# Projecting the MLP before the query: w3 ahead of wq, and x issued by ScalarE beside the first load

## The chip, the core and the metric

The kernel runs on one core of a Trainium2 chip. The metric is the device time of one execution in microseconds (us), median of several runs. A profile of one execution gives, for the same program, when each instruction started, what ended each wait, and every packet that the sixteen DMA engines of the core moved.

TensorE is PE in the profile, VectorE is DVE, ScalarE is ACT, GpSimd is POOL and SyncE is SP. PEld is the weight load of TensorE. A name with a q behind it (SPq, ACTq) is the sequencer of that engine, which issues DMAs and waits on semaphores.

## What is computed

One decoding step for two rows x of 1024 numbers, all in fp32. An attention branch with a long cache and an MLP branch are mixed by a gate:

```
g  = sigmoid((x * gate_w).sum(-1))
q  = x @ wq                                   # 1024 x 4096: 32 heads of 128
p  = softmax(q k^T * 128**-0.5)               # 4 key/value heads, 32768 positions, 2 batch rows
a  = (p v) @ wo                               # 4096 x 1024
b  = x1 + gelu(layernorm(x1) @ w3) @ w4       # w3 1024 x 3584, w4 3584 x 1024
out = g * a + (1 - g) * b
```

With a sequence of one, the spatial shift of the reference moves zeros in, so x1 is x, and w1 and w2 are not needed.

## The kernel before

The work is a stream of large loads through two buffers. `ring` holds two buffers of 64 KB in each of 128 partitions (8 MB each), called `flat[0]` and `flat[1]` when seen as flat rows. In order, they take wq in two halves, w3 in two halves, then for each of the eight pairs of batch row and key/value head the cache k in two halves and the cache v in two halves (`kt`, `vt`), with w4 in two halves after four pairs, and at the end wo. wq, k and v halves fill a buffer; a half of w3 or w4 takes seven eighths of one. What doesn't fit of wo goes to `tail`.

All these loads are issued by SP, one after the other. Before each, SP waits until the buffer that it overwrites has been read: `at("q0")`, `at("h0")`, `at("k0", m)` are counts on TensorE's semaphore that are reached when a half has been multiplied. A load is thus issued when TensorE is done with the load two places ahead of it, and runs behind the load that is then still under way in the other buffer.

The prologue (everything ahead of the eight pairs) is written out by hand, each engine's instructions in program order, with semaphores between them:

- The first two loads (`early`, L245) are issued by SP inside the tile context. Closing that context makes the engines meet twice at a barrier (L249). The next loads and all else come after it.
- x and gate_w lie in one small array `xg` (128 partitions of 96 bytes). Its DMA was issued by ACT behind the barrier (L278).
- When x has landed, DVE, PE and ACT work out the gate g, the layer norm and the padded operands: `x_pad` (x itself, for wq), `xn_pad` (the normed x, for w3) and `xr_pad` (x times 1 - g, which starts the sum in `acc`). The last of these on DVE is L338, `d_norm`.
- `project` multiplies one weight matrix, half by half, 32 matmuls a half. It takes the landing of a half off its semaphore and, when done with it, marks the semaphore for which SP waits. A float32 matmul stands as two records in the profile, so a half is 64.
- Before: q (x by wq), then the turn of q into columns (DVE L402 and L410, PE L416, DVE L424 and L427, which ends with `q_cur`, the operand of the first pair); then eight matmuls of `xr_pad` into `acc` (L434); then h (normed x by w3), its turn (L438 to L453) and the gelu (L457 to L469). Both turns go through the same buffers `row` and `p`.
- After the prologue the first pair multiplies `q_cur` by the first half of k as soon as that has landed (L488).

Of the kernel before, what the change touches and what calls it, by code (L numbers as in the profile page):

```python
# [14 lines left out]
P = 128  # L15
B, D, HQ, HKV, SK, DH, F = 2, 1024, 32, 4, 32768, 128, 3584
REP = HQ // HKV
PAIRS = B * HKV
# [8 lines left out]
PART = 2  # L27
HALF = P // PART
# [45 lines left out]
def kernel(  # L74
# [52 lines left out]
    nc = tc.nc  # L127
    scale = DH ** -0.5

    def new(name, *shape, parts=P):  # L130
        return nc.alloc_sbuf_tensor(name, [parts, *shape], F32).ap()

    def bank(name):
        return nc.alloc_psum_tensor(name, [P, 512], F32).ap()
# [3 lines left out]
    xg_sb = new("xg_sb", KD, 3)  # L138
    wide = new("wide", 3 * P)
    ones = new("ones", P)  # L140
    x_pad = new("x_pad", KD, C)
    xn_pad = new("xn_pad", KD, C)
    xr_pad = new("xr_pad", KD, C)
    q_pad = new("q_pad", PAIRS + 1, PART, 2, C)
    q_cur = new("q_cur", PART, 2, C)
# [19 lines left out]
    h = new("h", 2 * KF * B)  # L165
    u = new("u", 2 * KF * B)
# [5 lines left out]
    p = new("p", NI, NT, PART + 1, HALF)  # L172
# [4 lines left out]
    row = pt_all[:, 0]  # L177
# [6 lines left out]
    sc = [bank(f"sc{i}") for i in range(NI)]  # L184
    tr = [bank(f"tr{i}") for i in range(2)]
# [5 lines left out]
    compact = ident[:, ::C // B]  # L191
# [3 lines left out]
    def sem(name):  # L195
        cleared.append(nc.alloc_semaphore(name))
        return cleared[-1]

    stored = nc.alloc_semaphore("stored")
    pe, dve, act, pool = (Line(e, sem(n)) for e, n in (  # L200
        (nc.tensor, "pe"), (nc.vector, "dve"), (nc.scalar, "act"), (nc.gpsimd, "pool")))
    sp = Line(nc.sync)

    landed = [sem(f"landed{i}") for i in range(2)]
    w_in = [*landed, sem("w_in2")]
    got_x = sem("got_x")
# [10 lines left out]
    def load(dst, src, sem, *marks):  # L217
        sp.after(*marks)
        nc.sync.dma_start(dst, src).then_inc(sem, 16)

    def run(src, j):
        return src[PART * j:PART * (j + 1)].rearrange("i (q w) c -> (i q) (w c)", w=PART)

    flat = [t.rearrange("p w c -> p (w c)") for t in ring]

    PROLOGUE = ("run", "sum", "var", "q0", "q1", "qt", "h0", "h1", "ht")
    TURN = ("k0", "v0", "v1")
    STEP = ("s0", "s2", "s3", "mt", "bp", "tp00", "tp01", "tp02", "tp03", "tp10", "tp11", "tp12", "tp13", "lp", "op")  # L230

    def at(name, m=None):
        if m is None:
            return (pe.sem, 1 + PROLOGUE.index(name))
        return (pe.sem, len(PROLOGUE) + m * len(TURN) + m // 4 * 2 + 1 + TURN.index(name))

    def weighed(i):
        return (pe.sem, len(PROLOGUE) + 4 * len(TURN) + 1 + i)

    SUMMED = (pe.sem, len(PROLOGUE) + PAIRS * len(TURN) + 2 * 2)  # L240
    ENDED = (pe.sem, SUMMED[1] + 1)

    early = [nc.sync.dma_start(flat[j], run(wq, j)).then_inc(landed[j], 16) for j in range(2)]  # L245
    for inst in early:
        tc.no_tile_sem_insts.add(inst.ins.name)
    tc.close()
    tc.compile()  # L249

    load(flat[0][:, :PART * 2 * F], run(w3, 0), landed[0], at("q0"))
    load(flat[1][:, :PART * 2 * F], run(w3, 1), landed[1], at("q1"))

    half = PART * KF // 4
    STEPS = ((0, 14), (14, 9), (23, 5))
# [5 lines left out]
            load(flat[j][:, piece], run(src, j)[:, piece], landing, free[j])  # L261

    for m in range(PAIRS):
        free = [at("h" + "01"[j]) if m == 0 else at("v" + "01"[j], m - 1) for j in range(2)]
        if m == 4:
            weights(w4, ((0, half), (half, half)), *free)
            free = [weighed(0), weighed(1)]
        for j in range(2):
            load(flat[j], run(kt[m], j), landed[j], free[j])
        for j in range(2):  # L270
            load(flat[j], run(vt[m], j), landed[j], (at("k0", m), (k1_free, m + 1))[j])
    weights(wo, STEPS, at("v0", PAIRS - 1), at("v1", PAIRS - 1))
    load(tail[:, :2 * D], run(wo, 0)[:, half * D:], came[0][0])
    for mark, lo, hi in zip(came[1:], (0, 5, 7), (5, 7, 8)):
        load(tail[:, 2 * D + lo * D // G:2 * D + hi * D // G], run(wo, 1)[:, half * D + lo * D // G:half * D + hi * D // G], mark[0])


    nc.scalar.dma_start(xg_sb, xg).then_inc(got_x, 16)  # L278
    pool.mark(nc.gpsimd.memset(wide, 0.0))
    pool.after((pool.sem, pool.n))  # L280
    made = pool.mark(nc.gpsimd.affine_select(
        out=ident, in_=ident, pattern=[[-1, P]], base=0, channel_multiplier=1,
        compare_op=ALU.not_equal, fill=1.0))
# [17 lines left out]
    for i in range(2):  # L301
        last = nc.vector.tensor_copy(perm[:, :, i], ident.rearrange("p (q w) -> p w q", w=PART))
# [12 lines left out]
    for i in range(2):  # L315
        own = slice(i * HALF, (i + 1) * HALF)
        last = nc.vector.tensor_copy(
            x_run[own].rearrange("p (j w k) b -> p j w (k b)", j=2, w=PART),
            tr[1][own, :PART * KD * B].rearrange("p (w j i k b) -> p i j w (k b)", w=PART, j=2, i=2, b=B)[:, i])
    then(last)  # L320
    d_x = dve.mark(nc.vector.tensor_copy(x_pad[:, :, ::C // B], x_run))
# [10 lines left out]
    a_gate = act.mark(nc.scalar.activation(gate, tr[0][:, 0:B], AF.Sigmoid))  # L332
# [8 lines left out]
    for w in range(PART):  # L341
        last = nc.tensor.matmul(tr[1][:, w * KD * B:(w + 1) * KD * B], perm[:, w].rearrange("p i q -> p (i q)"), xs,  # L342
                                start=True, stop=True)
# [17 lines left out]
    def project(pad, n, banks):  # L361
        for T in range(4 // PART):
            pe.take(landed[T], 16)
            for kk in range(2 * PART):
                last = columns(flat[T], pad, 2 * PART * T + kk, kk, n, banks)
            done = pe.mark(last)
        return done
# [26 lines left out]
    def resumed():  # L394
# [1 line left out]
        return into_final(lambda half, which: spread[:, half * C:][:, :C],  # L396
                          lambda which, t: so_far[:, t * CHUNK:(t + 1) * CHUNK], (0, None), (1, None))

    pe.after(d_x)
    done = project(x_pad, HQ * DH, sc[0:2])  # L400
    dve.after(done)
    d_q = dve.mark(nc.vector.tensor_copy(row[:, 0], sc[0]))  # L402
    act.after(done)
    a_q = act.mark(nc.scalar.copy(row[:, 1], sc[1]))

    twice = p.rearrange("p i t w q -> p (i t w q)")[:, :REP * P * 2].rearrange(
        "p (h w i q) -> p h w i q", h=REP, w=PART, i=2)
    dve.after(d_q, a_q)
    for i in range(2):
        last = nc.vector.tensor_copy(twice[:, :, :, i], row.rearrange("p u (h q w) -> p (u h) w q", q=HALF, w=PART))  # L410
    d_twice = dve.mark(last)
    qt_ps = tr[0][:, :PART * HQ * B].rearrange("p (w h m) -> p w h m", w=PART, m=PAIRS)
    pe.after(d_twice, a_gate, made)
    for r in range(REP):
        for w in range(PART):
            last = nc.tensor.matmul(qt_ps[:, w, r], twice[:, r, w].rearrange("p i q -> p (i q)"), compact,  # L416
                                    start=True, stop=True)
    done = pe.mark(last)
    dve.after(done)
    for i in range(2):  # L420
        own = slice(i * HALF, (i + 1) * HALF)
        for s in range(2):
            lo = (2 * s + i) * REP
            last = nc.vector.tensor_copy(q_pad[own, :PAIRS, :, s, lo:lo + REP], qt_ps[own].rearrange("p w h m -> p m w h"))  # L424
    d_qt = dve.mark(last)
    dve.after(d_qt)
    d_q0 = dve.mark(nc.vector.tensor_copy(q_cur, q_pad[:, 0]))  # L427


    pe.after(d_norm)  # L430
    for k2 in range(2):
        for g in range(G):
            lo = P * (1 - k2)
            nc.tensor.matmul(acc[C * g:C * g + C], xr_pad[:, 2 * g + k2], wide[:, lo:lo + 2 * P],  # L434
                             start=(k2 == 0), stop=False, skip_group_check=True)
    done = project(xn_pad, F, sc[2:4])
    dve.after(done)
    d_h = dve.mark(nc.vector.tensor_copy(row[:, 0], sc[2]))  # L438
    act.after(done)
    a_h = act.mark(nc.scalar.copy(row[:, 1, :F // G - 512], sc[3][:, :F // G - 512]))  # L440
    n = KF // G
    both = p.rearrange("p i t w q -> p (i t w q)")[:, :n * P * 2].rearrange("p (c w i q) -> p c w i q", c=n, w=PART, i=2)
    dve.after(d_h, a_h, at("qt"))
    for i in range(2):
        last = nc.vector.tensor_copy(
            both[:, :, :, i], row.rearrange("p u n -> p (u n)")[:, :n * P].rearrange("p (c q w) -> p c w q", q=HALF, w=PART))
# [3 lines left out]
    for c in range(n):  # L450
        for w in range(PART):
            o = (c * PART + w) * PAIRS
            last = nc.tensor.matmul(ht_ps[:, o:o + PAIRS], both[:, c, w].rearrange("p i q -> p (i q)"), compact,  # L453
                                    start=True, stop=True)
    done = pe.mark(last)
# [10 lines left out]
    for i in range(2):  # L466
        for j in range(2):
            own = slice(i * HALF, (i + 1) * HALF)
            last = nc.vector.tensor_mul(  # L469
                w_pad[own, j * PART * n:(j + 1) * PART * n, ::C // B].rearrange("p (w c) b -> p w c b", w=PART),  # L470
                h[own].rearrange("p (c w j i b) -> p i j w c b", c=n, w=PART, j=2, i=2)[:, i, j],
                rest[own].rearrange("p (o z b) -> p o z b", o=1, z=1).to_broadcast([HALF, PART, n, B]))
    last.then_inc(x_in, 1)
    for landing in w_in[2:len(STEPS)]:
        nc.vector.sem_inc(landing, 16)
    assert pe.n == len(PROLOGUE)


# [85 lines left out]
    with nc.vector.Fori(0, PAIRS, 1) as m:  # L564
        turn_of = Turn(dve, own_step)
        for i in range(NI):
            if i != 1:
                nc.vector.wait_ge(*seen(f"s{i}"))
                if i == 3:
                    nc.vector.sem_inc(k1_free, 1)  # L570
                last = [nc.vector.reduce_max(out=mx[:, k:k + 1], in_=sc[k], axis=AX.X)  # L571
                        for k in ((1, 2) if i == 2 else (i,))][-1]
# [19 lines left out]
        for i in range(2):  # L592
            last = nc.vector.tensor_copy(pv_sb[:, :, :, i], pv.rearrange("p (s q w) -> p s w q", q=HALF, w=PART))  # L593
# [14 lines left out]
    for t, apart, lo, n in ((w_pad, C // B, 0, half), (o_last, 1, half, 2)):  # L608
        for i in range(2):
            own = slice(i * HALF, (i + 1) * HALF)  # L610
            for b in range(B):
                last = nc.vector.tensor_scalar_mul(
                    t[own, :, b * apart].rearrange("p (j c) -> p j c", c=n), o_by_block[own, i, :, lo:lo + n, b],
                    gate[own, b:b + 1])
# [61 lines left out]
```

## Time and profile before

| What | Value |
| --- | --- |
| median of 3 runs | 773.16 us (773.05 to 773.22) |
| profiled execution, first to last instruction (span) | 771.6 us |
| total of the profiled execution | not on the page |
| PE, DVE, ACT, POOL busy | 57%, 12%, 8%, 0% of the span |
| DMA queue of SP, share of 16 engines | 99.4% |
| bytes moved, mean rate | 331.50 MB, 430 GB/s |
| first two loads (wq), issue to landing | 21.9 and 40.8 us |
| load of x, issue to landing | 22.7 us, for 12 KB |

In the page of the profile the span is cut into 40 slices of 19.3 us. A row of digits gives the busy share of an engine in tenths for each slice, the row DMA that of the sixteen DMA engines, and the row GB/s what they moved. In the timeline, a line gives start, duration, engine, line of the kernel, operation, written and read tiles, and in brackets how long the engine had been idle and what ended it. In a table of stretches, the columns are the length of the stretch, then for each engine its busy time and number of instructions, then the granted clock of TensorE (PEclk), the share of time in which the DMA engines worked, and GB/s; a packet is counted whole where it starts, so that a short stretch in which packets start shows a share above one. The median of the runs is 1.6 us above the span of the profiled execution; what lies around the span isn't shown.

### The profile page before, as it was taken

How to read it: one execution, taken by the hardware profiler on the slowest of the kernel's cores; microseconds unless marked ns; L12 is line 12 of the kernel's file. 1: busy time of each engine (PE TensorE's matmuls, PEld its weight loads, DVE VectorE, ACT ScalarE, POOL GpSimd, SP SyncE). 2: the span in 40 equal slices, each digit the busy share in tenths (PEclk: the TensorE clock that was granted, in tenths of full speed). 3: DMA queues.
4: the chain of work that ended last, by engine and by line, in shares of the span. 5: the costliest groups of instructions: out<-in, count | busy, mean ns of one | idle time of the engine just before them, and what ended most of it. 6: DMA issues, size and time to landing. Idle time of an engine off the chain costs nothing. (4 is left out here: it accounts for less than half of the span.)

```text
span 771.6 us, 7439 instructions
## 1 busy us (share of the span) xinstructions
PE 436.4 (57%) x3332; PEld 199.9 (26%) x3332; DVE 95.2 (12%) x269; ACT 60.7 (8%) x144; POOL 3.8 (0%) x13
## 2 busy tenths in 40 slices
PE   0676746564645474546575446454745565646467
PEld 0232413232322232223233213121322232313134
DVE  1110202100210021002100002100210021002110
ACT  0000002000200020002000002000200020002000
POOL 1000000000000000000000000000000000000000
PEclk9977667767787768767766678777777677678788
DMA  9999999999999999999999999999999999999997
GB/s 381 435 436 436 435 436 435 436 436 431 428 431 431 435 435 435 435 435 435 430 428 440 432 435 435 435 435 435 435 435 435 431 431 435 431 435 431 431 424 327
DMA packets 6648, 331.50 MB, mean 430 GB/s; under 512 B 872, under 2 KB 1008, under 8 KB 1264
## 3 DMA queue, kind: packets, MB, share of 16 engines
q1 hardware_dynamic: 6496, 331.36, 99.4%
q8 instruction: 7, 0.11, 0.1%
q10 hardware_dynamic: 144, 0.01, 0.0%
q14 instruction: 1, 0.01, 0.0%
HBM read 331.36 MB, written 0.01 MB: 429 GB/s over the span
## 5 line engine op out<-in xcount | busy, mean ns | idle before, releaser
L488 PE MATMUL sc<-load,q_cur 128*32 128x512 f32 x1024 | 144.1, 722 | 132.3 <-PEq L53 132.3
L514 PE MATMUL pv<-load,pt 128*32 128x512 f32 x1024 | 134.2, 683 | 88.7 <-PEq L53 88.7
L488 PEld LDWEIGHTS sc<-load,q_cur 128*32 128x32 f32 x1024 | 51.2, 130 | 219.2 <-issue 214.8
L514 PEld LDWEIGHTS pv<-load,pt 128*32 128x32 f32 x1024 | 39.2, 124 | 173.9 <-issue 173.9
L505 PE MATMUL sc<-wide,p 128*128 128x128 f32 x256 | 44.5, 347 | 22.8 <-PEq L53 22.8
L571 DVE TENSOR_REDUCE mx<-sc 128x1 f32<-128x512 f32 x32 | 21.4, 689 | 284.8 <-PE sc L488 284.8
L555 ACT ACT_TABLE_LOAD x8 | 10.3, 1283 | 483.0 <-ACTq L53 483.0
L505 PEld LDWEIGHTS sc<-wide,p 128*128 128x128 f32 x256 | 40.1, 184 | 30.0 <-issue 30.0
L371 PE MATMUL acc<-load,w_pad 128*32 128x256 f32 x448 | 34.2, 478 | 18.9 <-PEq L53 18.9
L588 DVE COPY pt<-sc 64x256 f32<-64x256 f32 x64 | 25.9, 414 | 81.4 <-PE sc L505 80.9
L561 ACT COPY pt<-sc 64x256 f32<-64x256 f32 x64 | 23.5, 368 | 85.3 <-PE sc L505 83.0
L593 DVE COPY pv_sb<-pv 128x512 f32<-128x512 f32 x16 | 10.3, 686 | 145.6 <-PE tr L520 145.6
L371 PEld LDWEIGHTS acc<-load,w_pad 128*32 128x32 f32 x448 | 18.6, 137 | 33.6 <-issue 28.7
L524 PE MATMUL tr<-sel,pv_sb 128*128 128x8 f32 x128 | 18.9, 284 | 11.8 <-PEq L53 11.8
L555 ACT ACTIVATE p<-sc,bias 128x512 f32<-128x512 f32 x32 | 21.6, 686 | 0.1
L357 PE MATMUL sc<-load,x_pad 128*32 128x512 f32 x128 | 19.2, 768 | 4.1 <-PEq L53 4.1
L524 PEld LDWEIGHTS tr<-sel,pv_sb 128*128 128x128 f32 x128 | 18.4, 228 | 12.3 <-issue 12.3
L357 PE MATMUL sc<-load,xn_pad 128*32 128x384 f32 (+1 forms) x128 | 15.3, 641 | 7.9 <-PEq L53 7.9
L342 PE MATMUL tr<-xg_sb,perm 128*128 128x16 f32 x4 | 1.0, 372 | 25.2 <-DMA xg_sb<-xg 25.2
L584 DVE COPY p<-p 128x256 f32<-128x256 f32 x32 | 9.4, 294 | 26.7 <-ACT p L555 26.7
L357 PEld LDWEIGHTS sc<-load,xn_pad 128*32 128x32 f32 x128 | 4.8, 130 | 18.4 <-issue 18.4
L357 PEld LDWEIGHTS sc<-load,x_pad 128*32 128x32 f32 x128 | 4.9, 137 | 17.6 <-issue 17.5
(89 smaller groups left out, 96.3 us busy)
## 6 DMA issues: line engine op xcount, KB each, us to landing
load<-w SPq DMA_DIRECT2D x4, 7168.0 KB, 24.9
load<-wo SPq DMA_DIRECT2D x1, 7168.0 KB, 29.0
load<-wo SPq DMA_DIRECT2D x1, 4608.0 KB, 19.3
load<-wo SPq DMA_DIRECT2D x1, 2560.0 KB, 25.0
tail<-wo SPq DMA_DIRECT2D x1, 1024.0 KB, 27.0
tail<-wo SPq DMA_DIRECT2D x1, 640.0 KB, 28.1
load<-kt SPq DMA_DIRECT2D x16, 29.6
load<-vt SPq DMA_DIRECT2D x16, 29.5
```

Of the source, the lines that this page charges most:

```text
L357: last = nc.tensor.matmul(b[C * g:C * g + C, :hi - lo], pad[:, k], t[:, o + lo:o + hi], start=(k == 0), stop=(k == KD - 1))
L371: inst = nc.tensor.matmul(acc[C * g:C * g + C], lhsT, rows[:, g * (D // G):(g + 1) * (D // G)], start=False, stop=last, skip_group_check=True)
L488: last = nc.tensor.matmul(sc[i][C * g:C * g + C], q_cur[:, w, s], ring[j][:, w, o:o + 512], start=(s == 0 and w == 0), stop=(s == 1 and w ...
L505: last = nc.tensor.transpose(sc[k][:, t * P:(t + 1) * P], pair.rearrange("p w q -> p (w q)"), ident)
L514: last = nc.tensor.matmul(pv[C * g:C * g + C], pt[j][w][:, lo:lo + C], ring[j][:, w, o:o + G * DH], start=(j == 0 and w == 0 and t == 0), ...
L524: last = nc.tensor.matmul(tr[1][:, w * REP:(w + 1) * REP], pv_sb[:, s, w].rearrange("p i q -> p (i q)"), sel[:, s], start=(s == 0), stop=( ...
L555: nc.scalar.activation(p[:, i, :, :PART], sc[i].rearrange("p (t q w) -> p t w q", t=NT, w=PART), AF.Exp, bias=bias, scale=scale, accum_out ...
L561: nc.scalar.copy(*halves(1, j, c)).then_inc(pt_in, 1)
L571: last = [nc.vector.reduce_max(out=mx[:, k:k + 1], in_=sc[k], axis=AX.X) for k in ((1, 2) if i == 2 else (i,))][-1]
L584: nc.vector.tensor_copy(p[:, i, :, PART], p[:, i, :, 0]).then_inc(to_pe, 1)
L588: nc.vector.tensor_copy(*halves(0, j, c)).then_inc(pt_in, 1)
L593: last = nc.vector.tensor_copy(pv_sb[:, :, :, i], pv.rearrange("p (s q w) -> p s w q", q=HALF, w=PART))
```

## The change

Three things change, and no instruction is added or taken away but for one wait's place.

First, w3 is loaded into the two buffers at the start, and the two halves of wq follow when h has been multiplied. Second, the block that makes q and its turn moves behind the block that makes h, its turn and the gelu; the eight matmuls into `acc` come ahead of both. DVE's guard on the shared buffer moves with it: the later turn, now that of q, waits for `ht`, where the turn of h waited for `qt`. Third, the DMA of x is issued by ACT inside the tile context, ahead of its barrier.

```
-    PROLOGUE = ("run", "sum", "var", "q0", "q1", "qt", "h0", "h1", "ht")
+    PROLOGUE = ("run", "sum", "var", "h0", "h1", "ht", "q0", "q1", "qt")
...
-    early = [nc.sync.dma_start(flat[j], run(wq, j)).then_inc(landed[j], 16) for j in range(2)]
+    early = [nc.scalar.dma_start(xg_sb, xg).then_inc(got_x, 16),
+             *(nc.sync.dma_start(flat[j][:, :PART * 2 * F], run(w3, j)).then_inc(landed[j], 16) for j in range(2))]
...
-    load(flat[0][:, :PART * 2 * F], run(w3, 0), landed[0], at("q0"))
-    load(flat[1][:, :PART * 2 * F], run(w3, 1), landed[1], at("q1"))
+    load(flat[0], run(wq, 0), landed[0], at("h0"))
+    load(flat[1], run(wq, 1), landed[1], at("h1"))
...
-        free = [at("h" + "01"[j]) if m == 0 else at("v" + "01"[j], m - 1) for j in range(2)]
+        free = [at("q" + "01"[j]) if m == 0 else at("v" + "01"[j], m - 1) for j in range(2)]
...
-    nc.scalar.dma_start(xg_sb, xg).then_inc(got_x, 16)
...
-    pe.after(d_x)
-    done = project(x_pad, HQ * DH, sc[0:2])
...
     pe.after(d_norm)
...
     done = project(xn_pad, F, sc[2:4])
...
-    dve.after(d_h, a_h, at("qt"))
+    dve.after(d_h, a_h)
...
+    pe.after(d_x)
+    done = project(x_pad, HQ * DH, sc[0:2])
...
+    dve.after(d_q, a_q, at("ht"))
```

What ACT has at its start before: the branch into the block behind the barrier comes first, then the DMA of x.

```order
L672 UNCONDITIONAL_BRANCH [waits barrier_Pool_Activation_PE_DVE_SP_release]
L249 UNCONDITIONAL_BRANCH
L278 DMA xg_sb<-xg 128x24 [waits barrier_Pool_Activation_PE_DVE_SP_release]
L331 ACT_TABLE_LOAD
L331 ACTIVATE rstd<-rstd 128x2 [waits dve]
```

And after:

```order
L670 UNCONDITIONAL_BRANCH [waits barrier_Pool_Activation_PE_DVE_SP_release]
L245 DMA xg_sb<-xg 128x24
L250 UNCONDITIONAL_BRANCH
L331 ACT_TABLE_LOAD [waits barrier_Pool_Activation_PE_DVE_SP_release]
L331 ACTIVATE rstd<-rstd 128x2 [waits dve]
```

The DMA of x has moved ahead of the barrier, and nothing else on ACT has moved there.

What PE has between the small matmuls of the layer norm (L348) and the start of the h projection before (`x_pad` is x for wq, `xn_pad` the normed x for w3):

```order
L348 MATMUL tr<-part,ones 128x2 [waits dve]
L357 MATMUL sc<-load,x_pad 32x512 [waits landed0]
L357 MATMUL sc<-load,x_pad 32x512 x31
L357 MATMUL sc<-load,x_pad 32x512 [waits landed1]
L357 MATMUL sc<-load,x_pad 32x512 x31
L416 MATMUL tr<-wide,p 128x8 [waits pool,act,dve]
L416 MATMUL tr<-wide,p 128x8 x15
L434 MATMUL acc<-wide,xr_pad 32x256 x8
L357 MATMUL sc<-load,xn_pad 32x512 [waits landed0]
```

And after, from the same matmul to the first of the h projection:

```order
L348 MATMUL tr<-part,ones 128x2 [waits dve]
L403 MATMUL acc<-wide,xr_pad 32x256 [waits dve]
L403 MATMUL acc<-wide,xr_pad 32x256 x7
L357 MATMUL sc<-load,xn_pad 32x512 [waits landed0]
L357 MATMUL sc<-load,xn_pad 32x512 x3
L357 MATMUL sc<-load,xn_pad 32x384 x4
```

PE now has the matmuls into `acc` as its first work after the layer norm, and these wait for `xr_pad`; the first projection stands behind them. On SP the order of issue is the same but for the names: two halves of w3 ahead of the barrier (`load<-w`), two of wq behind it, each behind one wait on PE, then k.

More of the change, by code (lines that the diff above doesn't have):

```diff
@@ L397, in resumed @@
                           lambda which, t: so_far[:, t * CHUNK:(t + 1) * CHUNK], (0, None), (1, None))
-    pe.after(d_x)
-    done = project(x_pad, HQ * DH, sc[0:2])
[L401 to L427, printed above, removed]
     pe.after(d_norm)
@@ L475 @@
         nc.vector.sem_inc(landing, 16)
+    pe.after(d_x)
+    done = project(x_pad, HQ * DH, sc[0:2])
+    dve.after(done)
+    d_q = dve.mark(nc.vector.tensor_copy(row[:, 0], sc[0]))
+    act.after(done)
+    a_q = act.mark(nc.scalar.copy(row[:, 1], sc[1]))
+    twice = p.rearrange("p i t w q -> p (i t w q)")[:, :REP * P * 2].rearrange(
+        "p (h w i q) -> p h w i q", h=REP, w=PART, i=2)
+    dve.after(d_q, a_q, at("ht"))
+    for i in range(2):
+        last = nc.vector.tensor_copy(twice[:, :, :, i], row.rearrange("p u (h q w) -> p (u h) w q", q=HALF, w=PART))
+    d_twice = dve.mark(last)
+    qt_ps = tr[0][:, :PART * HQ * B].rearrange("p (w h m) -> p w h m", w=PART, m=PAIRS)
+    pe.after(d_twice, a_gate, made)
+    for r in range(REP):
+        for w in range(PART):
+            last = nc.tensor.matmul(qt_ps[:, w, r], twice[:, r, w].rearrange("p i q -> p (i q)"), compact,
+                                    start=True, stop=True)
+    done = pe.mark(last)
+    dve.after(done)
+    for i in range(2):
+        own = slice(i * HALF, (i + 1) * HALF)
+        for s in range(2):
+            lo = (2 * s + i) * REP
+            last = nc.vector.tensor_copy(q_pad[own, :PAIRS, :, s, lo:lo + REP], qt_ps[own].rearrange("p w h m -> p m w h"))
+    d_qt = dve.mark(last)
+    dve.after(d_qt)
+    d_q0 = dve.mark(nc.vector.tensor_copy(q_cur, q_pad[:, 0]))
     assert pe.n == len(PROLOGUE)
```

## The prediction, before the changed kernel was run

> **What bounds the kernel now.** I read the page first: the slices and the queues.
>
> ```profile
> PE   0676746564645474546575446454745565646467
> PEclk9977667767787768767766678777777677678788
> DMA  9999999999999999999999999999999999999997
> GB/s 381 435 436 436 435 436 435 436 436 431 428 431 431 435 435 435 435 435 435 430 428 440 432 435 435 435 435 435 435 435 435 431 431 435 431 435 431 431 424 327
> q1 hardware_dynamic: 6496, 331.36, 99.4%
> ```
>
> The DMA engines are busy in every slice; only the first slice and the last fall short of 435 GB/s, and the queue of SP fills 99.4% of sixteen engines. PE works about half the time. So the bytes set the time, and the change moves the same bytes. It can cost or bring time in one way: if it opens or closes a gap in the stream. I therefore read next what SP waits for, and the timeline of the prologue.
>
> ```profile
> SPq L219 <- PE sc L357: 82.3, 4, 35.7
> ```
>
> ```profile
> 0.73 0.87 SPq L245 DMA_DIRECT2D load<-wq  x2
> 2.39 0.37 ACTq L278 DMA_DIRECT2D xg_sb<-xg  x1
> ...
> 25.10 0.17 DVE L309 TENSOR_TENSOR xw<-xg_sb 128x16 f32<-128x16 f32 x1 [18.75 <-DMA xg_sb<-xg]
> ...
> 27.86 0.59 PE L348 MATMUL tr<-part,ones 128*128 128x2 f32 x2 [1.23 <-DVE part L327]
> ...
> 30.60 0.19 DVE L338 TENSOR_TENSOR xr_pad<-xg_sb,rest 128x16 f32<-128x16 f32 x1
> ...
> 38.09 14.03 SPq L219 DMA_DIRECT2D load<-w  x2
> 42.14 9.59 PE L357 MATMUL sc<-load,x_pad 128*32 128x512 f32 x64 [4.12 <-PEq L53]
> ...
> 60.63 1.94 PE L434 MATMUL acc<-wide,xr_pad 128*32 128x256 f32 x16
> 62.34 7.18 PE L357 MATMUL sc<-load,xn_pad 128*32 128x512 f32 x64
> 69.59 16.40 SPq L219 DMA_DIRECT2D load<-kt  x2
> ...
> 96.80 9.57 PE L488 MATMUL sc<-load,q_cur 128*32 128x512 f32 x64 [2.13 <-PEq L53]
> 106.42 18.60 SPq L219 DMA_DIRECT2D load<-vt  x2
> 116.15 8.43 PE L488 MATMUL sc<-load,q_cur 128*32 128x512 f32 x64 [9.79 <-PEq L53]
> ```
>
> The longest wait of SP, 35.7 us, is for the first projected half: x is late. It lands at 25.1; the first half of wq has been multiplied and the third load is issued at 38.09; the second half of wq, whose landing lets PE go on at 42.14, is still under way. The stream had about 4 us left when the next load joined it, and so has no gap. That margin is what the change moves.
>
> Why is x late? The packets tell. These stretches start where packets of the first load start.
>
> ```profile
> 0.00:1.75 1.75, 0.00 (x0) 0.00 (x0) 0.00 (x0) 0.00 (x0) 0.20 (x4) 1.00 0.00 0
> 1.75:2.15 0.40, 0.00 (x0) 0.00 (x0) 0.00 (x0) 0.00 (x0) 0.00 (x0) 1.00 7.97 2621
> 4.90:5.40 0.50, 0.00 (x0) 0.00 (x0) 0.50 (x2) 0.00 (x0) 0.50 (x4) 1.00 4.84 2097
> 7.30:7.80 0.50, 0.00 (x0) 0.00 (x0) 0.00 (x0) 0.00 (x0) 0.00 (x0) 1.00 4.86 2100
> 24.30:24.75 0.45, 0.00 (x0) 0.00 (x0) 0.00 (x0) 0.00 (x0) 0.00 (x0) 1.00 5.39 2330
> ```
>
> And the packet counts for 0 to 7 us, 7 to 8, 21 to 23 and 24 to 26, in this order; ahead of the last two lines, a round of the first kind (7 to 8) and one of w3 packets (46 to 48) by queue.
>
> ```profile
> DMA packets 32, 2.10 MB, mean 300 GB/s; under 512 B 0, under 2 KB 0, under 8 KB 0
> DMA packets 32, 1.05 MB, mean 1050 GB/s; under 512 B 16, under 2 KB 16, under 8 KB 16
> DMA packets 64, 1.05 MB, mean 526 GB/s; under 512 B 48, under 2 KB 48, under 8 KB 48
> DMA packets 32, 1.05 MB, mean 524 GB/s; under 512 B 16, under 2 KB 16, under 8 KB 16
> ...
> q1 hardware_dynamic: 16, 1.05, 241.8%
> ...
> q1 hardware_dynamic: 16, 0.92, 107.4%
> ```
>
> Each engine takes one large packet after another, in rounds of (24.30 - 4.90) / 8 = 2.42 us (the first took 4.90 - 1.75 = 3.15, so 0.75 of start-up). In the first two rounds there are 32 large packets and no small one. From the third on, sixteen small ones go with sixteen large ones: one packet of x per engine and round. With a closing packet, x needs nine turns; the round at 21 to 23 has two of them, since the closing packet of wq's first half makes one more turn. So x ends in the tenth round, at 24.3 to 24.75, and DVE goes on 0.35 later. x isn't slow because of its bytes but because it takes turns.
>
> **The change, part by part.** *The load of x, earlier.* ACT's DMA moves from 2.39 to about where SP's first stands, 0.73. From there to a first packet it is 1.75 - 0.73 = 1.02 us. x and the first half of w3 then reach the engines together. If x joins in the first or second round, its ninth turn falls in the ninth round (in the second case the extra turn makes up for the lost one). A packet of w3 is 0.92/1.05 of one of wq, so a round is 2.12 us: the ninth starts at 1.75 + 0.75 + 8 x 2.12 = 19.5 on the first engine, 19.9 on the last, and with 0.35 x is there at 20.2. That is 4.9 us earlier than before.
>
> The rule of the Trainium skill that speaks to this place is in DMA: Bandwidth & Descriptors, Queues, rings and completion order: an engine takes turns between queues but drains a whole packet of typically 9 to 17 descriptors from one before it switches. The counts above disagree: sixteen small ones per round is one per engine and turn. By that rule the nine of x would pass in one turn; this is rival 1 below.
>
> *w3 first.* Each half of w3 is eight rounds. The sixteenth ends at 1.75 + 0.75 + 16 x 2.12 = 36.4 on the first engine, 36.8 on the last. For wq the same sum gives 41.2; PE's wait at 42.14 fits. The stream thus needs its third load 4.8 us earlier than before.
>
> *The path from x to the third load.* From x to the end of `xr_pad` it is 30.60 + 0.19 - 25.10 = 5.7 us on DVE, ACT and PE, which the change leaves alone: 25.9. PE then has the matmuls into `acc` and the first half of h. Before, these ran back to back, from 60.63 to 62.34 + 7.18 = 69.52: 8.9 us, and SP issued 0.07 later. In the new order PE starts them after a pause, so its clock has to be looked at.
>
> ```profile
> 30.20:33.60 3.40, 3.40 (x24) 0.78 (x20) 1.00 0.71 308
> 33.60:37.00 3.40, 3.40 (x40) 0.93 (x35) 1.00 1.42 617
> ...
> 60.60:64.32 3.72, 1.98 (x12) 0.79 (x16) 0.50 0.64 278
> 64.32:69.55 5.23, 5.20 (x56) 1.44 (x48) 1.00 1.18 507
> ```
>
> These are the projections alone. The 8.9 us hold 3.7 at half clock (PEclk 0.50). The first projection of the kernel was slow from 27.86 to 33.60, 24 matmuls in 3.4 us against 40 in the next (the column says 1.00 there, the rate does not): 5.7 us. Half of a longer slow time is lost, so 8.9 to 9.9 us; I take 9.4. The third load is issued at 25.9 + 9.4 + 0.1 = 35.4 (34.9 to 35.9), its first packet can start 1.02 later, at 36.4 (35.9 to 36.9), and the stream ends at 36.4. The margin of 4 us is used up to nothing. The start-up of 0.75 was hidden under other packets in every later load. It is bare when a queue has run dry: the cost lies between 0 (the descriptors come 0.5 before the end and the start-up is covered) and 0.5 + 0.75 = 1.25. Nearest is the tie, with the start-up bare: 0.75.
>
> *The other loads.* The fourth load waits for the second half of h, which lands at about 37.2 and takes 9.4 us at most; the third is under way until 36.4 + 0.75 + 8 x 2.42 = 56.5. The first k load waits for the first half of q, 56.5 + 9.6 = 66.1, while the fourth runs to 76. None is late; cost nothing. If the gap above were longer, all move with it.
>
> *The turn of q, now last.* Before, the turn from the end of q to `q_cur` was:
>
> ```profile
> 51.80 0.69 DVE L402 COPY pt<-sc 128x512 f32<-128x512 f32 x1 [21.01 <-PE sc L357]
> ...
> 61.77 0.23 DVE L427 COPY q_cur<-q_pad 128x128 f32<-128x128 f32 x1
> ```
>
> That is 62.00 - 51.73 = 10.3 us. The second half of wq now lands one load of 8 x 2.42 = 19.4 us ahead of k. Projection and turn take 9.6 + 10.3 = 19.9. So the first pair may start 0.5 us after k has landed, not at once, and the load of v that waits for it is issued 0.5 later than 106.42. The load ahead of that one lets PE go on only at 116.15; cover 9 us, cost nothing. The gelu, which was 2 us ahead of the first pair, now lies under the loads of wq. The moved guard waits for the turn of h, which ends some 30 us before it is asked; the buffers it guards are free. ACT's table load comes 0.4 us earlier and waits for nothing new.
>
> Sum: 0.75 us of gap on the profiled execution's span of 771.6. The median is 773.16; with the 1.6 us around the span unchanged, 773.9.
>
> **The rivals.**
> 1. *x goes through at once.* If ACT's descriptors reach the engines before SP's, or pass in one turn, x is there by about 5 us, and the first half of h waits for w3 instead, whose closing packet falls in the ninth round too, so 20.2. With 9.4 us at most it is done at 29.6, and the third load can start at 30.7, 5.7 us before the stream needs it. Time 773.2, as before. For it: DMAs of 0.37 and 0.40 us that start together. Against: one small packet a round, in every round seen.
> 2. *x misses a round more (slower).* Before, x was issued at 2.39, could start at 3.41, and still was not in the round at 4.90: an engine had settled its next packet before. If on any one engine the same happens to a packet of x that comes just behind w3's first, x starts in the third round, and ends in the tenth: 21.6 to 22.0, plus 0.35 gives 22.3. The third load is issued 15.2 us later, at 37.5, starts at 38.5 (38.0 to 39.0) and the gap is 2.1 + 0.75 = 2.9 (2.2 to 3.4). Time 776.0 (775.3 to 776.6). It decides once x is ready later than the choice of the second packet, between 1.75 and 3.41.
> 3. *x gains only its issue time.* With 22.7 us from issue to landing as before, x lands at 23.4; the gap is 3.2 + 0.75 = 4.0 and the time 777.1. Against it: a round is now 2.12 and not 2.42.
>
> **How the numbers follow.** The tie (forecast) 0.46, own range 773.1 to 774.5; rival 1 0.17; rival 2 0.29; rival 3 0.03; something not seen that closes a gap, 0.05. A difference under 0.2% (1.55 us) can hardly be told from none. The tie and rival 1 are within it, less 0.03 for a wrong estimate of the path: same 0.60. Slower: 0.29 + 0.03 + 0.03 = 0.35. Faster 0.05. The range takes in rival 1 and nearly all of rival 2: 772.9 to 776.6.
>
> **What would show it.** x landing at about 20.2 (DVE L309) with first small packets in round one or two; the third load's issue at 35.4; a row of packets that ends at 36.4 to 36.8 and starts again at most 1.3 us later; no other gap; first k matmul half a microsecond behind its landing. The prediction is wrong if x lands at 22 or later, or if the path from x is shorter than the 15.2 us I added up, by so much that no gap is left.

## The result and the profile after

The changed kernel takes 774.56 us (median of 21 runs, 773.93 to 775.16); the kernel before, 773.16 (21 runs, 772.99 to 773.48). The ratio is 1.0017, 95% interval 1.0011 to 1.0023: 1.4 us slower, and just under the 0.2% that I had called the edge of what can be told. The profiled execution took 774.31 us, with a span of 772.8 against 771.6. One execution of the kernel before, among those of the experiments, took 791.15 us at a granted clock of 0.557 and is left out of every comparison.

The page of the changed kernel, slices and SP's queue:

```profile
DMA  9999999999999999999999999999999999999997
GB/s 380 434 435 432 434 432 435 432 432 431 434 434 434 434 434 434 434 434 434 430 427 443 432 434 434 434 431 434 434 434 434 434 434 434 434 434 434 420 426 321
q1 hardware_dynamic: 6496, 331.36, 99.3%
```

The stream still fills the time; nothing on the page shows a gap of a microsecond. The timeline and the packets of the changed kernel do. First the timeline, read as the chain that the prediction added up:

```profile
0.73 0.39 ACTq L245 DMA_DIRECT2D xg_sb<-xg  x1
0.73 0.88 SPq L246 DMA_DIRECT2D load<-w  x2
...
20.54 0.18 DVE L309 TENSOR_TENSOR xw<-xg_sb 128x16 f32<-128x16 f32 x1 [14.17 <-DMA xg_sb<-xg]
...
26.03 0.18 DVE L338 TENSOR_TENSOR xr_pad<-xg_sb,rest 128x16 f32<-128x16 f32 x1
26.27 1.94 PE L403 MATMUL acc<-wide,xr_pad 128*32 128x256 f32 x16 [2.39 <-DVE xr_pad L338]
27.98 7.21 PE L357 MATMUL sc<-load,xn_pad 128*32 128x512 f32 x64
35.26 8.71 SPq L219 DMA_DIRECT2D load<-wq  x2
...
94.38 0.23 DVE L473 COPY q_cur<-q_pad 128x128 f32<-128x128 f32 x1
97.30 9.23 PE L486 MATMUL sc<-load,q_cur 128*32 128x512 f32 x64 [3.98 <-PEq L53]
```

x is there at 20.54, the third load is issued at 35.26, and the first half of k lets PE start at 97.30 where it was 96.80. Around the third load, the packets of the changed kernel start in these stretches:

```profile
34.20:34.75 0.55, 0.55 (x12) 0.12 (x4) 0.00 (x0) 0.00 (x0) 0.00 (x0) 1.00 3.85 1668
34.80:36.30 1.50, 0.39 (x8) 0.00 (x0) 0.00 (x0) 0.00 (x0) 0.00 (x0) 1.00 0.00 0
36.30:37.30 1.00, 0.00 (x0) 0.00 (x0) 0.00 (x0) 0.00 (x0) 0.00 (x0) 1.00 2.93 1049
37.30:39.30 2.00, 1.92 (x20) 0.81 (x24) 0.00 (x0) 0.00 (x0) 0.00 (x0) 1.00 0.00 0
39.30:40.00 0.70, 0.70 (x12) 0.32 (x8) 0.00 (x0) 0.00 (x0) 0.00 (x0) 1.00 3.46 1498
```

The last packets of w3 start from 34.2, the first of wq from 36.3, the next from 39.3: a round of 3.0 us where a packet of 64 KB takes 2.42. The spread of the sixteen engines also goes from half a microsecond to nearly one in that round: w3's last packet ends at 36.82, but three engines begin wq only between 37.17 and 37.25. The start-up is bare, and some engines stood idle.

In the kernel before, the third load was issued 3.1 us ahead of the end of wq. Its first packets, those of w3, all start in the half microsecond in which the packets of wq end:

```profile
41.20:41.65 0.45, 0.00 (x0) 0.00 (x0) 0.00 (x0) 0.00 (x0) 0.00 (x0) 0.50 4.75 2039
```

### The profile page after: what moved, and what is told of

The parts are those of the page before. It is cut to its first block, busy times and chain, and to the rows that moved or that the text cites. A ratio compares the mean times of both kernels' runs of the same rounds, so it can differ in the third digit from the quotient of the medians.

```text
span 772.8 us, 7439 instructions
## 1 busy us (share of the span) xinstructions
PE 431.5 (56%) x3332; PEld 194.7 (25%) x3332; DVE 95.2 (12%) x269; ACT 60.7 (8%) x144; POOL 3.8 (0%) x13
## 5 line engine op out<-in xcount | busy, mean ns | idle before, releaser
L486 PE MATMUL sc<-load,q_cur 128*32 128x512 f32 x1024 | 146.8, 735 | 134.6 <-PEq L53 134.6
L512 PE MATMUL pv<-load,pt 128*32 128x512 f32 x1024 | 132.6, 677 | 88.9 <-PEq L53 88.9
L486 PEld LDWEIGHTS sc<-load,q_cur 128*32 128x32 f32 x1024 | 48.3, 132 | 227.0 <-issue 224.5
L357 PE MATMUL sc<-load,xn_pad 128*32 128x384 f32 (+1 forms) x128 | 13.4, 574 | 2.2 <-PEq L53 2.2
L493 PE MATMUL tr<-wide,m 128*1 128x128 f32 x8 | 2.2, 269 | 9.7 <-PEq L53 9.7
```

The costliest lines, as they stand in the source:

```text
L357: last = nc.tensor.matmul(b[C * g:C * g + C, :hi - lo], pad[:, k], t[:, o + lo:o + hi], start=(k == 0), stop=(k == KD - 1))
L486: last = nc.tensor.matmul(sc[i][C * g:C * g + C], q_cur[:, w, s], ring[j][:, w, o:o + 512], start=(s == 0 and w == 0), stop=(s == 1 and w ...
L512: last = nc.tensor.matmul(pv[C * g:C * g + C], pt[j][w][:, lo:lo + C], ring[j][:, w, o:o + G * DH], start=(j == 0 and w == 0 and t == 0), ...
```

## The experiments

All were compared with runs of the kernel before on the same chip (its median was 773.12 to 773.22). "Third load" is SP's first issue at L219; the changed kernel has it at 35.26. The first edit is shown against the kernel before, the others against the changed kernel unless said otherwise. The trace does not name the engine of a packet; what is said of single engines is read from which packet begins where another ends.

**One half of the change: x early, wq first.**

```
-    early = [nc.sync.dma_start(flat[j], run(wq, j)).then_inc(landed[j], 16) for j in range(2)]
+    early = [nc.scalar.dma_start(xg_sb, xg).then_inc(got_x, 16),
+             *(nc.sync.dma_start(flat[j], run(wq, j)).then_inc(landed[j], 16) for j in range(2))]
...
-    nc.scalar.dma_start(xg_sb, xg).then_inc(got_x, 16)
```

> Only the load of x moves (inside the context, beside the first load); wq stays first. Theory gap: x takes its nine turns among packets of 2.42 us and lands at about 22.2 instead of 25.1, the third load is issued at about 35, 6 us before the stream ends at 41.6; no gap, 773.2 us (773.0 to 773.4). Rival crowded start (ACT and SP issuing together spreads the sixteen engines, and the slowest engine keeps that): 773.5 to 774.0, with first packets spread over 0.6 us instead of 0.35. Rival late q (the loss comes from wq and the turn of q standing last): 773.2.

773.14 us, ratio 1.0000 (0.9991 to 1.0009). Its timeline:

```profile
22.99 0.17 DVE L309 TENSOR_TENSOR xw<-xg_sb 128x16 f32<-128x16 f32 x1 [16.62 <-DMA xg_sb<-xg]
35.16 0.33 SPq L219 DMA_DIRECT2D load<-w  x1
```

The third load is issued as early as in the changed kernel, but here the stream has work until 41.1, so it costs and brings nothing. Issuing x together with the first load costs nothing either: the first packets do start over 0.8 us here, against 0.3 before, but the time is that of the kernel before, so the crowded start falls. x landed 0.8 later than expected.

**The other half: w3 first, x behind the barrier as before.**

```
-    early = [nc.scalar.dma_start(xg_sb, xg).then_inc(got_x, 16),
-             *(nc.sync.dma_start(flat[j][:, :PART * 2 * F], run(w3, j)).then_inc(landed[j], 16) for j in range(2))]
+    early = [nc.sync.dma_start(flat[j][:, :PART * 2 * F], run(w3, j)).then_inc(landed[j], 16) for j in range(2)]
...
+    nc.scalar.dma_start(xg_sb, xg).then_inc(got_x, 16)
```

> Only the order moves (w3 and h first); x is issued by ACT behind the barrier as before. Theory gap: first small packets in the third round, x lands at about 22.4, third load issued at about 37.3 and first packets at 38.3 against a stream that ends at 36.4; gap 1.9 and bare start-up 0.5 to 0.75: 775.7 us (775.2 to 776.5). Rival crowded start: no crowd here, so no more than 773.5. Rival late q: as the changed kernel, 774.6.

775.59 us (5 runs, 775.52 to 776.88), ratio 1.0038 (1.0024 to 1.0052). x at 22.33, third load at 37.07. Its packets:

```profile
34.10:34.60 0.50, 0.50 (x8) 0.12 (x4) 0.00 (x0) 0.00 (x0) 0.00 (x0) 1.00 4.23 1835
36.30:37.95 1.65, 1.39 (x20) 0.34 (x12) 0.00 (x0) 0.00 (x0) 0.00 (x0) 1.00 0.01 0
38.00:38.95 0.95, 0.95 (x16) 0.47 (x12) 0.00 (x0) 0.00 (x0) 0.00 (x0) 1.00 3.30 1104
38.95:41.00 2.05, 2.05 (x27) 0.79 (x20) 0.00 (x0) 0.00 (x0) 0.00 (x0) 1.00 0.00 0
41.00:41.85 0.85, 0.85 (x16) 0.40 (x12) 0.00 (x0) 0.00 (x0) 0.00 (x0) 1.00 2.74 1176
```

w3's last packets, 2.12 us each, end between 36.3 and 36.7. Nothing large starts until 38.0, and the round after that takes 3.0. The gap is now in plain sight; the cost comes from w3 first, and the earlier x takes back 1.0 to 1.5 us of it (the changed kernel's two medians are 774.56 and, further down, 774.13).

**The matmuls into acc behind the h projection.**

```
-    pe.after(d_norm)
-    for k2 in range(2):
...
+    pe.after(d_xn)
     done = project(xn_pad, F, sc[2:4])
+    pe.after(d_norm)
+    for k2 in range(2):
...
```

> The changed kernel, but the eight matmuls into acc come behind the h projection, which then waits for xn_pad (1.5 us earlier than xr_pad) instead. Theory gap: the third load is issued 2.5 to 3.3 us earlier, at 32 to 32.8, joins a running stream, no gap, no bare start-up: 773.2 us (772.9 to 773.4), 1.4 under the changed kernel. Rival crowded start: x still joins with the first load, so 773.6 to 774.6. Rival late q: 774.6, since q is as late.

773.31 us (773.12 to 773.62, and one of the eleven runs at 775.05), ratio 1.0005 (0.9995 to 1.0014). The third load is issued at 33.32. Its packets start on time:

```profile
34.10:34.80 0.70, 0.00 (x0) 0.00 (x0) 0.00 (x0) 0.00 (x0) 0.00 (x0) 1.00 3.02 1311
36.20:36.90 0.70, 0.00 (x0) 0.00 (x0) 0.00 (x0) 0.00 (x0) 0.00 (x0) 0.50 3.65 1498
38.70:39.80 1.10, 1.10 (x9) 0.25 (x5) 0.00 (x0) 0.00 (x0) 0.00 (x0) 0.50 2.20 953
```

The rounds are 2.1 and then 2.5 apart. The order of w3 and wq and the place of x are those of the changed kernel, so neither is the cost in itself: the late q falls too. What had made the third load late enough to cost 1.4 us, with w3 first, is eight small matmuls, and a wait for their operand, ahead of the work that frees a buffer. Why one run of eleven took 1.7 us longer than their median was not seen.

**Smaller packets beside x.** The first half of w3 in four pieces, by columns; `project` then waits for all four:

```
...
+             *(nc.sync.dma_start(flat[0][:, o:o + F], run(w3, 0)[:, o:o + F]).then_inc(landed[0], 16)
+               for o in range(0, PART * 2 * F, F)),
...
```

> The changed kernel, but the first half of w3 is loaded in four pieces by columns, packets of 14 KB in place of 57 KB. Theory turns (x is late because each of its packets waits for one large one): x lands at about 7 us (nine turns of 0.53 us), h waits for its own half at 20 instead, third load issued at 28 to 30, no gap: 773.2 us (772.9 to 773.4). Rival, x is held by the bytes ahead of it in time and not by turns: x at about 20 again, third load at 35.3, 774.6. Rival crowded start: x at 7 but still 773.6 to 774.6.

773.32 us, ratio 1.0002 (0.9993 to 1.0011); third load at 28.55. The issues of its DMAs (KB each, us to landing):

```profile
load<-w SPq DMA_DIRECT2D x4, 1792.0 KB, 12.5
load<-w SPq DMA_DIRECT2D x1, 7168.0 KB, 34.5
xg_sb<-xg ACTq DMA_DIRECT2D x1, 12.0 KB, 7.0
```

In the changed kernel the row of x was

```profile
xg_sb<-xg ACTq DMA_DIRECT2D x1, 12.0 KB, 19.8
```

The same 12 KB of x among the same bytes land in 7.0 us instead of 19.8. x waits for turns, and a turn is as long as the packet next to it.

**x ahead of w3 on SP's own queue.**

```
-    early = [nc.scalar.dma_start(xg_sb, xg).then_inc(got_x, 16),
+    early = [nc.sync.dma_start(xg_sb, xg).then_inc(got_x, 16),
```

> The changed kernel, but SP issues x itself, ahead of the first half of w3, on the same queue. Theory turns: x stands ahead of the large packets in one queue and takes no turns, so it lands at 2.5 to 4 us; h waits for w3 instead, third load issued near 29, no gap; the stream starts one issue (0.4 us) later: 773.5 us (773.2 to 773.8). Rival, small packets of 96 bytes are slow in themselves: x lands near 20 and the time is 774.6 or more.

773.71 us, ratio 1.0009 (1.0000 to 1.0018). Its issue row:

```profile
xg_sb<-xg SPq DMA_DIRECT2D x1, 12.0 KB, 1.9
```

Without turns x needs 1.9 us. The first load is issued 0.46 later for it (1.19 against 0.73), so the stream starts that much later; the time is 0.58 longer, 0.1 more than that.

**Eight more matmuls ahead of h**, of the same shape as those into acc, into an unused bank:

```
+    for k2 in range(2):
+        for g in range(G):
+            nc.tensor.matmul(pv[C * g:C * g + C, :2 * P], xr_pad[:, 2 * g + k2], wide[:, :2 * P],
+                             start=(k2 == 0), stop=(k2 == 1))
```

> The changed kernel with eight more matmuls of 128x256 ahead of the h projection, whose result is not used. Theory gap: x lands as in the changed kernel (20.5), but the third load is issued 0.9 to 1.7 us later, at 36.2 to 37, and the time grows by as much: 775.5 to 776.3 us, as with the late x of w3 first alone, which had 37.07. Rival, the cost lies in x's place among the packets: 774.6.

774.86 us (773.80 to 775.49), ratio 1.0021 (1.0012 to 1.0030): less than expected, and nearer to the rival's 774.6. The changed kernel on the same chip took 774.13, though (further down), so the eight matmuls cost 0.7 us. In the profiled execution, which took 775.39, x came at 20.60 as in the changed kernel and the third load at 37.02; the first packets of wq start only here:

```profile
37.50:37.95 0.45, 0.00 (x0) 0.00 (x0) 0.00 (x0) 0.00 (x0) 0.00 (x0) 1.00 0.00 0
37.95:38.35 0.40, 0.00 (x0) 0.00 (x0) 0.00 (x0) 0.00 (x0) 0.00 (x0) 1.00 7.77 2621
```

That is the gap of w3 first alone, with x on time: the issue of the third load counts, not the place of x. The profiled execution is among the longest of the eleven; how late the others issued was not seen.

**Half of the matmuls into acc behind h**, the other four ahead:

```
+            if k2 == 0:
...
+    for g in range(G):
+        nc.tensor.matmul(acc[C * g:C * g + C], xr_pad[:, 2 * g + 1], wide[:, 0:2 * P],
+                         start=False, stop=False, skip_group_check=True)
```

> The changed kernel with four of its eight matmuls into acc behind the h projection. Theory gap with start-up: the third load is issued 0.4 to 0.9 us earlier, at 34.4 to 34.9, its first packet could start at 35.4 to 35.9, ahead of the stream's end at 36.4 to 36.9. If a join before the end is free: 773.2 to 773.5 us. If the start-up needs about 3 us of lead (with all acc matmuls behind h and a lead of 3.1, one engine still began 0.9 late): 773.6 to 774.2.

774.31 us, ratio 1.0016 (1.0007 to 1.0025). It missed: the time lies above both expectations. Its timeline tells why:

```profile
27.17 8.71 PE L357 MATMUL sc<-load,xn_pad 128*32 128x512 f32 x64
35.95 8.07 SPq L219 DMA_DIRECT2D load<-wq  x2
```

With less work ahead, h started 0.8 earlier than in the changed kernel but took 8.71 us instead of 7.21; the third load was issued 0.7 later. Four records of h take 0.64 to 0.85 us up to 32.2, and 0.32 to 0.43 from there; in the changed kernel that came at 30.0. So the step was smaller than what the clock of TensorE does to it. The expectation also says that with all matmuls into acc behind h one engine began 0.9 late; the packet records of that run show all sixteen beginning wq within a few ns of the end of their last w3 packet, and four of these first packets taking 2.8 to 3.0 us.

**The changed kernel again.**

> The changed kernel once more, on the chip of these three, for its spread: 774.6 us (773.9 to 775.2). In its profile the shift of the large packets after the third load is 0.4 to 1.2 us against the kernel before; what the end shows beyond that comes from which engine carries the 16 KB instruction packets, and differs from execution to execution. Rival, the end shift of 1.2 us is a fixed cost of the new order: 1.2 again, on whichever engine.

774.13 us (773.80 to 775.33), ratio 1.0016 (1.0007 to 1.0025). In this execution:

```profile
28.22 7.49 PE L357 MATMUL sc<-load,xn_pad 128*32 128x512 f32 x64
35.78 8.45 SPq L219 DMA_DIRECT2D load<-wq  x2
```

The same program issued its third load 0.5 later than in the first profile. From the packet records, the mean start of a round well behind the third load (at 78 us) is 0.95 us later than before in this one, and 0.57 in the first. The end moves by what the slowest engine does: the last data come 1.0 later than before here, 1.2 in the first. So the two executions come to nearly the same end by different ways, and two profiles can't tell whether that end is a fixed cost of the order. The first profile's half microsecond beyond its gap lies in the engines drifting apart. Seven instruction packets of 16 KB (the kernel before has as many) each hold up one engine by 1.2 to 1.5 us: the packet takes about 1.0, and the data packet behind it up to 0.5 longer than 2.42. In the first profile the slowest engine's start is 0.75 later than before at 361 us and 1.20 at 477; between them two such packets fall, and the one at 431 us hit an engine that was already behind most.

**A busy TensorE ahead of h.** 105 unused matmuls ahead of x's landing and 20 behind the layer norm:

```
+    pe.after(made)
+    for _ in range(105):
+        nc.tensor.matmul(pv[:, :256], ident, wide[:, :256], start=True, stop=True)
...
+    for _ in range(20):
+        nc.tensor.matmul(pv[:, :256], ident, wide[:, :256], start=True, stop=True)
```

> The changed kernel with 105 unused matmuls of 128x256 on PE ahead of x's landing (about 6 to 20 us) and 20 more between the layer norm's last matmul and those into acc, so that PE is never at rest. Theory clock: PE's clock is full when h starts, acc and h take 7.0 us instead of 8.9 to 9.6, the third load is issued at about 33.4, a lead of 3 us, and the time is 773.2 to 773.5, with a spread over runs as small as that of the kernel before (0.5 us) instead of 1.2 to 1.5. Rival, the third load's lateness doesn't hang on the clock at the start of h: issue at 35.3 or later, 774.1 to 774.6.

807.74 us, ratio 1.0444 (1.0430 to 1.0458): I had sized the fillers by matmuls of 32 columns, but these take 0.44 us and held PE until 51. What it does show is acc and half of h at full clock (granted 1.00 from 8.3 us on), 62.44 to 69.59, 7.1 us:

```profile
62.44 1.07 PE L408 MATMUL acc<-wide,xr_pad 128*32 128x256 f32 x16
63.33 7.05 PE L360 MATMUL sc<-load,xn_pad 128*32 128x512 f32 x72
69.59 0.33 SPq L219 DMA_DIRECT2D load<-wq  x1
```

**The same with 32 and 5 fillers, twice.**

> As the kernel with 105 and 20 unused matmuls, whose 0.44 us each held PE until 51 us, but with 32 ahead of x's landing (until about 19) and 5 behind the layer norm's last matmul. Theory clock: acc and the first half of h take 7.1 us as there (62.44 to 69.54), not 8.9 to 9.6; the third load is issued at 33.3 to 33.8, about 3 us ahead of the stream's end; 773.2 to 773.5 us, spread over runs 0.5 instead of 1.2 to 1.5. Rival, the third load's lateness doesn't hang on the clock: issue at 35.3 or later, 774.1 to 774.6.

> The kernel with 32 and 5 unused matmuls once more, for a second profile. If its clock drops again at the start of h: issue at 34 to 35 and the large packets late by about 1 us. If the clock stays full: acc and half of h in 7.1 us, issue at 33.3 to 33.8. Theory free join: then no loss at the third load. Rival lead: a loss of a few tenths even so.

774.87 us (773.99 to 775.41), ratio 1.0020 (1.0011 to 1.0029), and 775.06 (773.90 to 775.60), ratio 1.0023 (1.0012 to 1.0033). The first expectation missed, in the issue and in the time. In the second profile the clock dropped again (0.50 from 23.2 to 26.6 us), and the issue came as expected for that case, with the large packets 1.4 late. Stretches of the first one's profile:

```profile
24.50:26.50 2.00, 2.00 (x6) 1.46 (x5) 0.36 (x2) 0.78 (x2) 0.00 (x0) 0.50 1.06 459
...
36.30:37.00 0.70, 0.00 (x0) 0.00 (x0) 0.00 (x0) 0.00 (x0) 0.00 (x0) 1.00 2.68 843
37.00:39.00 2.00, 0.55 (x4) 0.23 (x8) 0.00 (x0) 0.00 (x0) 0.00 (x0) 0.68 0.64 229
39.20:41.50 2.30, 2.30 (x20) 0.81 (x16) 0.00 (x0) 0.00 (x0) 0.00 (x0) 0.58 1.07 456
```

The clock fell to half (0.50) in the layer norm, which has little for PE, and the fillers behind it ran slowly, so that acc and h took 7.3 and 7.1 us but began at 27.0 and 27.2. The third load came at 34.35 and 34.38, 0.9 ahead of the changed kernel and some 2 us ahead of the stream's end, and still cost more: in the first, one engine began it as late as 38.9; in the second, its first packets took up to 4.3 us. Why these two join worse than the changed kernel with a later issue is not settled. They differ in that an instruction packet of 16 KB falls at 32 us, in the rounds just ahead. With eight more matmuls one fell at 36.5 and did no such harm, but there the stream had run dry around it, so that doesn't decide it.

**acc behind h, and four unused matmuls ahead of h**, shown against the kernel with acc behind h:

```
+    for g in range(G):
+        nc.tensor.matmul(pv[C * g:C * g + C, :2 * P], x_pad[:, g], wide[:, :2 * P], start=True, stop=True)
     done = project(xn_pad, F, sc[2:4])
```

> The kernel with the matmuls into acc behind h, and four unused matmuls of 128x256 ahead of h: the third load is issued 0.4 to 0.9 us later than there, at about 34.0 (33.7 to 34.6), a lead of 2 to 2.6 us on the end of the stream. Theory free join (a load issued more than 1.7 us ahead costs nothing): 773.2 to 773.5 us, first packets of the third load at 2.4 us each. Rival lead (a load needs some 3 us ahead, less is paid in part): 773.6 to 774.6, first packets of 2.6 to 3.3 us and some engines idle, as with the short fillers, where an issue at 34.35 still cost 1.2.

773.70 us (773.05 to 774.89), ratio 1.0010 (1.0001 to 1.0019). In the profiled execution, 773.93, the third load was issued at 33.83 and joined without a pause:

```profile
34.00:34.85 0.85, 0.00 (x0) 0.00 (x0) 0.00 (x0) 0.00 (x0) 0.00 (x0) 1.00 2.49 1079
36.10:37.00 0.90, 0.00 (x0) 0.00 (x0) 0.00 (x0) 0.00 (x0) 0.00 (x0) 0.57 2.77 1165
38.50:39.85 1.35, 1.35 (x15) 0.32 (x11) 0.00 (x0) 0.00 (x0) 0.00 (x0) 0.50 1.80 777
```

A lead of 2.3 us on the end of the stream (36.1) was enough here: the mean start of the round at 78 us is 0.05 us behind that of the kernel before, and twelve of the sixteen first packets took 2.5 us or less. In this execution, then, the theory of the free join holds, and a lead of 3 us was not needed. The times don't settle it: the median of 773.70 lies above the theory's 773.5 and within the rival's range. The span was 772.4, with the mean round at 719 us 0.1 late and the slowest engine 0.6: what it lost, it lost in engines that drift apart. Its executions range over 1.8 us, seven up to 773.93 and four from 774.62 on; whether those four missed the join was not seen.

Read together by the issue of the third load, the profiled executions agree in the main, the fillers apart, and x on SP's queue, which starts the whole stream later:

| Third load | Kernel | Span |
| --- | --- | --- |
| 28.55 | small first packets | 771.8 |
| 33.32 | acc behind h | 771.8 |
| 33.83 | the same, four matmuls ahead | 772.4 |
| 35.26 and 35.78 | changed kernel | 772.8 and 772.6 |
| 35.95 | half of acc behind h | 773.0 |
| 37.02 | eight more matmuls | 773.9 |
| 37.07 | w3 first alone | 774.1 |

Up to 33.3, 0.2 us at most is lost against 771.6; from 35.3 to 37.1 the span grows by 1.3 us for 1.8 us of delay, though not step by step: the later of the changed kernel's two has the shorter span.

## Why the prediction was right

The direction and the mechanism held: 773.9 forecast, 774.56 measured, within the range. The range, 772.9 to 776.6, was wide enough that the time alone could hardly have missed it; the steps say more. By its steps:

- *x at 20.2.* It was 20.54. Its small packets come in the second round, one per engine: in the changed kernel the stretch 4.4 to 5.1 us has

```profile
DMA packets 32, 0.92 MB, mean 1313 GB/s; under 512 B 16, under 2 KB 16, under 8 KB 16
```

  16 of 32 small, so rivals 1 and 2 fell here. The ninth turn came in the ninth round, as reckoned. From issue to landing x took 19.8 us, and with w3 first but x behind the barrier 19.9. So the earlier issue gained just its earlier start, 1.8 us, and the rest of the 4.6 came from the shorter packets. That is rival 3's mechanism; I had reckoned it with the old landing time and put it at 777. The Trainium skill says that issuing from several engines at once only saves the time that the sequencer takes to issue (DMA: Bandwidth & Descriptors, Issuing engines are not separate DMA queues). The run with x on SP's own queue agrees: without ACT's help SP's first load is issued 0.46 us later, and the stream starts that much later.
- *The path of 15.2 us and the third load at 35.4.* 14.7 us and 35.26 in the first profile, 15.0 and 35.78 in the second. Its term of 9.4 for acc and h measured 8.9 and 9.2.
- *The stream's end at 36.4 and the tie.* w3's last packets end from 36.3; the tie it was.
- *A gap of 0.75 us.* As the mean delay of the rounds it was about right: they came 0.57 later in the first profile and 0.95 in the second, on either side of it. That was partly luck, since I had taken it as the nearest value between 0 and 1.25. As the whole cost it was too small: in the medians the cost was 1.4 us, and 1.0 when the kernel was run again. Two things were left out. I took the mid of the slow stretch of TensorE as if it were one number, while the issue of the same program moved from 35.26 to 35.78. And I took a gap for the whole cost, while the end waits for the slowest of sixteen engines: 1.2 and 1.0 at the end of the two profiles.
- *The turn of q, 0.5 us after k.* It was done 2.7 us before PE started on k (94.61 and 97.30); the transposes took 4.6 us, not 6.8. No consequence, as foreseen.

The spread of runs, 1.2 us against 0.5 before, goes with it: the first half of h took 7.21, 7.49 and 8.71 us in three executions whose work for it is the same, depending on when the clock rose: h became fast at 30.0, 30.8 and 32.2 us. The Trainium skill gives the reason that the clock is set by a free-running window of about 3.4 us (TensorE: Matmul & The Clock Gate, Part 1: The HAM clock gate). The trace agrees: in the first profile the granted clock changes at 30.03, 47.09, 64.16 and 70.99 us, five, five and two times 3.41 apart. That this alone makes the spread of the runs was not shown: with the short fillers acc and h took 7.3 and 7.1 us in the profiled executions, and the runs still spread over 1.4 and 1.7 us. Where the third load had ample lead, with x early only and with small first packets, the spread was 0.3 and 0.4 us.

No version here beats the kernel before. With w3 first, two undo the loss by an earlier third load, acc behind h and small first packets, both at 773.3; with wq first there is no loss to undo. In all of these the stream of bytes is the bound.

## What to carry to other kernels

Where one queue of loads is the bound, look at every issue for its lead on the end of the load before, and count a smaller load ahead of it as less lead: w3 ahead of wq moved no byte and added no work, but took away 4.8 us of cover from a path that was shortened by 2.8 only. On the path to an issue, put nothing that the issue doesn't need; eight matmuls that could wait made the difference. A small load beside large ones pays one large packet per turn; cut the packets beside it, or put it ahead in the same queue, which delayed the stream here by one issue.

## What was not expected of the hardware

A load issued 0.5 to 2.0 us ahead of the stream's end did not join it cleanly: with an issue at 34.35, five engines that were free began their first packet some 1.0 to 2.3 us late, and with one at 33.83 all were on time within 0.2 us. And a single 16 KB instruction packet holds up one of sixteen engines by 1.2 to 1.5 us. In the first profile the slowest engine's delay against the kernel before stayed at 1.2 us from 477 us to the end; that the packet at 431 us alone made it so was argued from the order of starts, not tested.
